# Hash attention and maxout FFN: scaling on GpSimd, one parity copied by VectorE, products of 32 columns with sums and hash in one burst, even pace, first pair by head

## The chip, the cores and the metric

The kernel runs on one core of a Trainium2 chip. The metric is the device time of one execution in microseconds, as the median of three runs: 338.43 us before the change (338.42 to 340.52). Engines are named as in the profile: PE (TensorE matmuls), PEld (its weight loads), DVE (VectorE), ACT (ScalarE), POOL (GpSimd), SP (SyncE, which here only issues DMAs).

## The reference

Attention masked by a hash, then a feed-forward network (FFN) with a maximum over three products. Batch 4, 8 heads, sequence 768, head dimension 64, six hash bits.

```python
q_bits = (np.einsum('bhsd,dk->bhsk', q, proj) > 0)      # k_bits alike
mask = q_bucket[:, :, :, None] == k_bucket[:, :, None, :]
scores = scale * np.matmul(q, k.transpose(0, 1, 3, 2))
scores = np.where(mask, scores, -1000000000.0)
attn = np.exp(scores - np.max(scores, axis=-1, keepdims=True))
attn = attn / (np.sum(attn, axis=-1, keepdims=True) + 1e-09)
attn_out = np.matmul(attn, v)
x = attn_out.transpose(0, 2, 1, 3).reshape(B * S, H * D)     # 3072 x 512
h = np.maximum(np.maximum(x @ w1, x @ w2), x @ w3)           # 3072 x 768
out = h @ w_out                                              # 3072 x 512
```

A query whose bucket holds no key of its own gets the mean of all values; the kernel has this by adding a tiny EPS times the sum of all values to the numerator and EPS times S to the denominator.

## The kernel before, in words

**Pairs.** Two heads make a pair; there are 16 pairs, four to a batch. For each pair q, k and v (384 KB each) are loaded by SP (`load`, L101, and `load_v`, L110). The sequence lies in "parity" order: a transposition (L140) puts the 64 dimensions of even chunks on partitions 0 to 63 and of odd chunks on 64 to 127.

**Preparation of a pair** (`prep_groups`, L123). Four transposition groups (`tgroup`), one for each side (q or k) and head, of three PE transposes into a PSUM tile mp and one DVE copy into T2 (L143, L145). Then `hashes` (L155): four fp32 products with the projection pj into bp, each 32 columns wide (L160), a DVE comparison to bits of +-0.5 (L163), and four small DMAs that put the bits under the dimensions in the tile S (L169). S holds 64 dimensions and 6 bits for both parities in bf16: POOL casts the even parity from T2 (L173), and an SBUF-to-SBUF DMA issued by POOL brings the odd one (L174). For pair 0 ACT writes S instead (L150, L152).

**Scores.** A unit is a pair, half of its queries, a pair of key chunks and a head: 192 units, 12 to a pair, 48 to a batch. `scores` (L221) makes two products of 70 rows into sc, and ACT takes the exponential into one of twelve fp16 tiles AT (L229). sc has two buffers, so the scores of a unit wait for the exponential of two units earlier. The bits add so much to a score that the exponential of a pair of different buckets vanishes.

**Values.** After six units (half of a pair's queries) `values` (L231) runs a burst on PE: twelve products of 64 columns into av (L237; the 385th column, of ones, gives the sum of the values), twelve of 32 columns with `ones` into sm, the denominators (L244). DVE copies both to SBUF (avs L250, ys L251). av has one buffer; sm, mp, bp and the FFN's l share three buffers named ms.

**Normalization** (`normalize`, L256), in steps at fixed distances in units after the burst: gather (at once; two SP DMAs bring the sums to dd, L271, and POOL scales the sum of the values by EPS into sv, L272), invert (6 units later; DVE adds and takes the reciprocal, and POOL issues a DMA to DRAM, rd, L275 to L278), spread (9; POOL issues two broadcasts rb, L282), scale (15 and 16; DVE computes (avs + sv) * rb into xT, L286). For the last pair of a batch each half is normalized by itself, otherwise both together.

**FFN** (`ffn_groups`, L180). For each half of a batch 18 groups of four products (three weights, six blocks of 128 columns; L190) with a DVE copy or maximum into ht (L195, L197), then three groups of six products into the output (L203), an ACT copy (L206) and an SP DMA (L208).

**Order.** All engines run their instructions in the order in which the loop at L306 emits them. For a unit u it emits in turn the loads, casts and weights that are due, the scores of u + 1, preparation, FFN groups, the burst of the six units before (one unit late), and the due steps. Preparation and FFN are paced by credits: a unit earns 0.40 of preparation (0.28 after the first batch) and 0.65 of FFN; a transposition group costs 0.34, a hash 0.82, an FFN group 0.66 or 1.32. Preparation may be up to six pairs ahead. Weights are issued by POOL at units 14, 21, 28 and 35 (L120). The FFN of a batch enters 12 units into the next. What is left runs after the loop (L338).

Of the kernel before, what the change touches and what calls it, by code (L numbers as in the profile page):

```python
# [17 lines left out]
def kernel(  # L18
# [82 lines left out]
    def load(pi):  # L101
        b, jj = divmod(pi, HPAIR)
        nats = []
        for nm, src in (("qnat", q), ("knat", k)):
            t = nat.tile([P, 2, NCH * D], FP32, tag=nm, name=nm)
            nc.sync.dma_start(t[:], src[b, 2 * jj : 2 * jj + 2].rearrange("h (p c) d -> p h (c d)", p=P))
            nats.append(t)
        natural[pi] = nats
# [14 lines left out]
    def prep_groups(pi):  # L123
        st = {}

        def begin():
            st["T2"] = t2pool.tile([P, 2, 2, HALF], FP32, tag="T2", name="T2")
            st["S"] = spool.tile([KR, 2, 2, 2, HALF], BF16, tag="S", name="S")
            trans[pi] = st["S"]
            if 2 <= pi + 2 < NPAIR:  # L130
                load(pi + 2)

        def tgroup(side, hd):
            def go():
                if not st:
                    begin()
                mp = ms_ps.tile([P, 512], FP32, tag="ms", name="mp")
                n = natural[pi][side]
                for i in range(CH2):
                    nc.tensor.transpose(mp[:, i * P : (i + 1) * P], n[:, hd, 2 * i * D : (2 * i + 2) * D], iden[:])  # L140
                o = st["T2"][:, side, hd, :]
                if side == 0:
                    nc.vector.tensor_scalar(out=o, in0=mp[:, 0:HALF], scalar1=QS, scalar2=None, op0=AluOp.mult)  # L143
# [11 lines left out]
        def hashes():  # L155
            bp = ms_ps.tile([P, 512], FP32, tag="ms", name="bp")
            for side in range(2):
                for hd in range(2):
                    g = 2 * side + hd
                    nc.tensor.matmul(bp[32 * g : 32 * g + 32, 0:HALF], pj[:, :], st["T2"][:, side, hd, :],  # L160
                                     start=True, stop=True)
            bits = bpool.tile([P, HALF], BF16, tag="bits", name="bits")
            nc.vector.tensor_scalar(out=bits[:], in0=bp[:, 0:HALF], scalar1=0.0, scalar2=0.5,  # L163
                                    op0=AluOp.is_gt, op1=AluOp.subtract)
            for hd in range(2):
                for side in (1, 0):
                    p0 = 32 * (2 * side + hd)
                    eng = nc.scalar if pi == 0 and side else nc.sync
                    eng.dma_start(st["S"][D:KR, side, hd, :, :], bits[p0 : p0 + 2 * NBITS, :])  # L169
            if pi > 0:  # L170
                so = st["S"][0:D].rearrange("d s h par w -> d (s h) par w")
                t2 = st["T2"].rearrange("p s h w -> p (s h) w")
# [3 lines left out]
        gs = [(0.34, tgroup(s, h), pi) for h in (0, 1) for s in (1, 0)]  # L176
        gs += [(0.82, hashes, pi)]
        return gs

# [38 lines left out]
    WEIGHTS_AT = (14, 21, 28, 35)  # L218
# [12 lines left out]
    def values(g):  # L231
# [15 lines left out]
        if qh == 0:  # L247
            avs_of[pi] = avspool.tile([P, 2, HALF + 4], FP32, tag="avs", name="avs")
# [7 lines left out]
    def normalize(pi, q0, nq):  # L256
# [8 lines left out]
        sv = small.tile([P, 1], FP32, tag="sv", name="sv")  # L265
# [3 lines left out]
        def gather():  # L269
            for half in range(2):  # L270
                nc.sync.dma_start(dd[:, half, 0:W], ys[32 * half : P : D, q0 : q0 + nq, :])  # L271
            nc.gpsimd.tensor_scalar_mul(sv[:], avs[:, q0, HALF : HALF + 1], EPS)  # L272

        def invert():
            nc.vector.scalar_tensor_tensor(out=rr[:, 0:W], in0=dd[:, 0, 0:W], scalar=EPS * S, in1=dd[:, 1, 0:W],  # L275
                                           op0=AluOp.add, op1=AluOp.add)
# [8 lines left out]
        def scale(i):  # L285
            return lambda: nc.vector.scalar_tensor_tensor(  # L286
                out=xt[:, jj, (q0 + i) * HALF : (q0 + i + 1) * HALF], in0=avs[:, q0 + i, 0:HALF],
                scalar=sv[:], in1=rb[:, i, :], op0=AluOp.add, op1=AluOp.mult)

        return [(0, gather), (6, invert), (9, spread)] + [(15 + i, scale(i)) for i in range(nq)]  # L290

    with tc.manual_schedule():
        load(0)
        cast_v = {0: load_v(0)}
        load(1)
        for _, g, _ in prep_groups(0):
            g()
        cast_v[0]()
        cast_v[1] = load_v(1)

        prep, ffn, steps = [], [], []
        p_credit = f_credit = 0.0
        for p2 in range(1, NPAIR):
            prep += prep_groups(p2)
        scores(0)
        for u in range(NU):  # L306
            pi = units[u][0]
            b, ub = divmod(u, UPB)
            if u % UPP == 2 and pi + 2 < NPAIR:
                cast_v[pi + 2] = load_v(pi + 2)  # L310
            if u % UPP == 8 and pi + 1 < NPAIR:
# [3 lines left out]
            if ub == 12 and b > 0:  # L315
# [19 lines left out]
        steps = [(0.85 * (n - NU), g) for n, g in steps]  # L335
        steps += [(1.35 * n, g) for n, g in values(NU // UPG - 1)]
# [35 lines left out]
```

## Time and profile before

| | |
|---|---|
| median of 3 runs | 338.43 us |
| the profiled execution's own time | 335.21 us |
| its span, first to last instruction | 333.4 us |
| mean granted TensorE clock | 0.977 |
| PE busy | 300.6 us (90%) |
| DVE busy | 180.0 us (54%) |
| ACT busy | 184.0 us (55%) |
| POOL busy | 88.4 us (27%) |
| bytes moved by DMA | 38.84 MB |

The span is cut into 40 slices in the page's second part, each digit a busy share in tenths. A group line gives busy time, the mean length of one instruction, and the idle time of the engine ahead of it with what ended it. A wait line reads: engine and line, what it waited for, total, times, longest. The chain follows the work that ended last backwards, each step to what released it.

### The profile page before, as it was taken

The page shows a single profiled execution, that of the slowest core. Times are in us where ns is not written, and L with a number is a line of the kernel's source. Part 1 is how long each engine was busy: PE and PEld are TensorE (multiplying, and loading weights), DVE is VectorE, ACT ScalarE, POOL GpSimd, SP SyncE. Part 2 cuts the span into 40 slices and gives each one's busy share as a digit, 9 for nine tenths or more (in the row PEclk, how much of TensorE's full clock was granted, in tenths as well). Part 3 has the DMA queues.
Part 4 walks back from the last instruction along what each step waited for, and adds up shares of the span by engine and source line. Part 5 has one row for each costly group of instructions (what it writes and reads, how often), then busy time and mean ns, then how long its engine had stood idle before and what let it go on. Part 6 is the DMA issues. An engine that isn't in the chain of part 4 may idle for free.

```text
span 333.4 us, 5887 instructions
## 1 busy us (share of the span) xinstructions
PE 300.6 (90%) x2192; PEld 159.2 (48%) x2192; DVE 180.0 (54%) x377; ACT 184.0 (55%) x225; POOL 88.4 (27%) x136
## 2 busy tenths in 40 slices
PE   1599993798877999999999999999999999999994
PEld 1165542253433555556545554455455545546561
DVE  1245660555425665476726674376355627768480
ACT  1576574076680567766474656777777676420202
POOL 0033272263541232323532132122313030321000
PEclk9999998599997999999999999999999999999998
DMA  5458979989783444454443214323431030141202
GB/s 179 158 192 148 214 176 230 194 255 157 251 156 94 82 139 90 163 137 129 81 114 71 52 51 108 115 49 79 104 108 46 5 139 7 50 118 27 96 0 94
DMA packets 32059, 38.84 MB, mean 117 GB/s; under 512 B 8464, under 2 KB 27936, under 8 KB 32032
## 3 DMA queue, kind: packets, MB, share of 16 engines
q1 hardware_dynamic: 22988, 25.94, 25.2%
q0 software_dynamic: 9008, 12.52, 21.3%
q8 instruction: 17, 0.28, 0.4%
q14 instruction: 10, 0.08, 0.1%
q10 hardware_dynamic: 36, 0.02, 0.0%
HBM read 31.46 MB, written 6.39 MB: 114 GB/s over the span
## 4 chain that ended last, share of the span: by engine, by line
PE 74%; DMA 11%; ACT 5%; DVE 3%; issue 3%; POOL 2%; SPq 1%; ACTq 0%; DVEq 0%; POOLq 0%
PE l L190 28%; PE sc L226 15%; PE av L237 10%; PE l L203 8%; PE sm L244 5%; DMA rb<-rd 4%; ACT AT L229 4%; PE bp L160 4%; PE mp L140 4%; DMA dd<-ys 3%; DMA rd<-rr 2%; DMA knat<-in_k_dram 1%; DVE T L145 1%; DMA S<-bits 1%; ACT osb L206 1%
## 5 line engine op out<-in xcount | busy, mean ns | idle before, releaser
L229 ACT ACTIVATE AT<-sc,bias_t 128x768 f16<-128x768 f32 x192 | 167.1, 906 | 98.9 <-PE sc L226 89.5
L190 PE MATMUL l<-xT,w_sb 128*128 128x384 f16 x576 | 111.2, 327 | 2.4 <-DVE T L145 2.4
L226 PE MATMUL sc<-S 70*128 70x384 bf16 x384 | 92.8, 330 | 11.2 <-ACT AT L229 7.5
L190 PEld LDWEIGHTS <-w_sb 128*128 128x128 f16 x576 | 55.5, 97 | 43.6 <-issue 8.2
L197 DVE TENSOR_TENSOR ht<-ht,l 128x384 f16<-128x384 f16 x96 | 53.1, 553 | 20.1 <-PE l L190 16.6
L226 PEld LDWEIGHTS <-S 70*128 70x128 bf16 x384 | 34.6, 98 | 51.5 <-issue 29.9
L195 DVE CAST ht<-l 128x384 f16<-128x384 f32 x48 | 26.7, 556 | 32.5 <-PE l L190 31.9
L278 POOL DMA_DIRECT2D rd<-rr x20 | 13.7, 684 | 115.1 <-DVE rr L277 115.1
L237 PE MATMUL av<-AT,vo 128*64 128x385 f16 x384 | 39.3, 341 | 0.0
L173 POOL CAST S<-T 64x1536 bf16<-64x1536 f32 x15 | 22.2, 1480 | 58.9 <-DVE T L143 56.5
L206 ACT COPY osb<-l 128x512 f32<-128x512 f32 x24 | 14.2, 590 | 39.6 <-PE l L203 39.6
L203 PE MATMUL l<-wout_sb,ht 128*128 128x512 f16 x144 | 34.2, 379 | 0.3 <-DVE ht L197 0.3
L250 DVE COPY avs<-av 128x385 f32<-128x385 f32 x32 | 17.9, 560 | 26.2 <-PE av L237 26.2
L282 POOL DMA_DIRECT2D rb<-rd x40 | 21.7, 545 | 30.5 <-DMA rd<-rr 28.9
L145 DVE COPY T<-mp 128x384 f32<-128x384 f32 x32 | 17.8, 555 | 21.9 <-PE mp L140 20.8
L286 DVE SCALAR_TENSOR_TENSOR xT<-avs,sv,rb 128x384 f16<-128x384 f32 x32 | 19.5, 612 | 18.2 <-DMA rb<-rd 18.2
L237 PEld LDWEIGHTS <-vo 128*64 128x64 f16 x384 | 19.6, 112 | 18.5 <-issue 10.8
L160 PE MATMUL bp<-T,pj 128*32 128x384 f32 x128 | 19.6, 542 | 7.4 <-DVE T L143 7.2
L140 PE MATMUL mp<-iden,knat 128*128 128x128 f32 x96 | 17.2, 291 | 6.9 <-DMA knat<-in_k_dram 6.9
L244 PE MATMUL sm<-AT,ones 128*32 128x384 f16 x384 | 21.6, 332 | 0.0
L203 PEld LDWEIGHTS <-ht 128*128 128x128 f16 x144 | 13.9, 97 | 15.8 <-DVE ht L197 1.1
L143 DVE TENSOR_SCALAR T<-mp 128x384 f32<-128x384 f32 x32 | 17.7, 552 | 6.2 <-PE mp L140 6.0
(28 smaller groups left out, 126.8 us busy)
## 6 DMA issues: line engine op xcount, KB each, us to landing
qnat<-in_q_dram SPq DMA_DIRECT2D x16, 384.0 KB
knat<-in_k_dram SPq DMA_DIRECT2D x16, 384.0 KB
vnat<-in_v_dram SPq DMA_DIRECT2D x16, 384.0 KB
out_dram<-osb SPq DMA_DIRECT2D x24, 256.0 KB
rb<-rd POOLq DMA_DIRECT2D x24, 192.0 KB, 3.5
S<-T POOLq DMA_DIRECT2D x15, 192.0 KB, 4.1
w_sb<-in_moe_w_dram POOLq DMA_DIRECT2D x3, 768.0 KB, 10.3
rb<-rd POOLq DMA_DIRECT2D x16, 96.0 KB, 3.0
```

What stands on the lines that cost most here:

```text
L140: nc.tensor.transpose(mp[:, i * P : (i + 1) * P], n[:, hd, 2 * i * D : (2 * i + 2) * D], iden[:])
L160: nc.tensor.matmul(bp[32 * g : 32 * g + 32, 0:HALF], pj[:, :], st["T2"][:, side, hd, :], start=True, stop=True)
L173: nc.gpsimd.tensor_copy(so[:, :, 0, :], t2[0:D])
L190: nc.tensor.matmul(ps[:, 0:HALF], w_sb[wi][:, jc, fb * P : (fb + 1) * P], xb[:, jc, hf * HALF : (hf + 1) * HALF], start=(jc == 0), stop=(j ...
L195: nc.vector.tensor_copy(hts[fb][:], ps[:, 0:HALF])
L197: nc.vector.tensor_tensor(out=hts[fb][:], in0=hts[fb][:], in1=ps[:, 0:HALF], op=AluOp.max)
L203: nc.tensor.matmul(ps[:, 0:DM], hts[fb][:, tb * P : (tb + 1) * P], wout_sb[:, fb, :], start=(fb == 0), stop=(fb == NFB - 1))
L226: nc.tensor.matmul(sc[:, j, 0:HALF], th[0:KR, 1, hd, j, kp * P : (kp + 1) * P], th[0:KR, 0, hd, qh, :], start=True, stop=True)
L229: nc.scalar.activation(at[:, :, 0:HALF], sc[:, :, 0:HALF], ActFn.Exp, bias=bias_t[:], scale=SCALE)
L237: nc.tensor.matmul(av[hd * D : (hd + 1) * D, 0 : HALF + 1], vones[pi][:, hd, c * D : (c + 1) * D], ats[2 * (c // 2) + hd][:, c % 2, 0 : HA ...
L244: nc.tensor.matmul(sm[32 * t : 32 * t + 32, 0:HALF], ones[:, :], ats[2 * (c // 2) + hd][:, c % 2, 0:HALF], start=(s == 0), stop=(s == CH2 ...
L282: nc.gpsimd.dma_start(rb[hd * D : (hd + 1) * D, 0:nq, :], rd[hd : hd + 1, 0 : nq * HALF].to_broadcast((D, nq * HALF)))
```

## The change

- The product with rb and the sum with sv: sv is now made by DVE from av itself (one column), added as a per-partition scalar in the copy of av to avs; the constant for the denominators is added in the copy of sm to ys. The product avs * rb moves to POOL (`tensor_mul`).
- The odd parity of S is copied by DVE from T2 instead of by a DMA.
- The av products are 24 of 32 columns instead of 12 of 64. A hash that is ready is emitted between the sm products and the copies of the burst, so it stands on PE right after sm, and on DVE its bits and its parity copy stand ahead of sv, avs and ys.
- Pace: one transposition group in each of the first four units of six until the FFN begins, then one in every third unit; FFN credit 0.66; FFN from 9 units into a batch; weights at units 18, 28, 38, 48; v loaded one pair ahead, not two; steps at 0, 6, 8, 10.
- Pair 0: its loads are cut by head and k comes first; proj is issued by ACT instead of by SP ahead of q and k; hash, bits and their DMAs run by head. In every pair k is loaded ahead of q.

```diff
-    for par in range(2):
-        nc.sync.dma_start(pst[par * D : (par + 1) * D, :], proj[:, :])
-        nc.vector.tensor_copy(pj[par * D : (par + 1) * D, par : 2 * NBITS : 2], pst[par * D : (par + 1) * D, :])
+    def load_proj():
+        for par in range(2):
+            nc.scalar.dma_start(pst[par * D : (par + 1) * D, :], proj[:, :])
+            nc.vector.tensor_copy(pj[par * D : (par + 1) * D, par : 2 * NBITS : 2], pst[par * D : (par + 1) * D, :])
...
+        for h0, nh in ((0, 1), (1, 1)) if pi == 0 else ((0, 2),):
+            for side in (1, 0):
+                h = 2 * jj + h0
+                nc.sync.dma_start(nats[side][:, h0 : h0 + nh, :],
+                                  (q, k)[side][b, h : h + nh].rearrange("h (p c) d -> p h (c d)", p=P))
...
+            if pi == 0:
+                for hd in hds:
+                    for side in range(2):
+                        p0 = 32 * (2 * side + hd)
+                        nc.vector.tensor_scalar(out=bits[p0 : p0 + 32, :], in0=bp[p0 : p0 + 32, 0:HALF], scalar1=0.0,
+                                                scalar2=0.5, op0=AluOp.is_gt, op1=AluOp.subtract)
+                        (nc.sync, nc.scalar)[side].dma_start(st["S"][D:KR, side, hd, :, :],
+                                                             bits[p0 : p0 + 2 * NBITS, :])
+                return
...
-                nc.gpsimd.tensor_copy(so[:, :, 0, :], t2[0:D])
-                nc.gpsimd.dma_start(so[:, :, 1, :], t2[D : 2 * D])
+            nc.gpsimd.tensor_copy(so[:, :, 0, :], t2[0:D])
+            nc.vector.tensor_copy(so[:, :, 1, :], t2[D : 2 * D])
...
+        if pi == 0:
+            return [tgroup(1, 0), tgroup(0, 0), lambda: hashes((0,)), tgroup(1, 1), tgroup(0, 1), lambda: hashes((1,))]
+        return [tgroup(s, h) for h in (0, 1) for s in (1, 0)], hashes
...
-    WEIGHTS_AT = (14, 21, 28, 35)
+    WEIGHTS_AT = (18, 28, 38, 48)
+    FFN_AT = 9
...
-                nc.tensor.matmul(av[hd * D : (hd + 1) * D, 0 : HALF + 1], vones[pi][:, hd, c * D : (c + 1) * D],
-                                 ats[2 * (c // 2) + hd][:, c % 2, 0 : HALF + 1], start=(c == 0), stop=(c == NCH - 1))
+                for vh in range(2):
+                    p0, d0 = hd * D + 32 * vh, c * D + 32 * vh
+                    nc.tensor.matmul(av[p0 : p0 + 32, 0 : HALF + 1], vones[pi][:, hd, d0 : d0 + 32],
+                                     ats[2 * (c // 2) + hd][:, c % 2, 0 : HALF + 1], start=(c == 0), stop=(c == NCH - 1))
...
+        if hash_ready:
+            hash_ready.pop(0)()
...
-        nc.vector.tensor_copy(avs_of[pi][:, qh, 0 : HALF + 1], av[:, 0 : HALF + 1])
-        nc.vector.tensor_copy(ys_of[pi][:, qh, :], sm[:, 0:HALF])
+        sv = small.tile([P, 1], FP32, tag="sv", name="sv")
+        nc.vector.tensor_scalar(out=sv[:], in0=av[:, HALF : HALF + 1], scalar1=EPS, scalar2=None, op0=AluOp.mult)
+        nc.vector.tensor_scalar(out=avs_of[pi][:, qh, :], in0=av[:, 0:HALF], scalar1=sv[:], scalar2=None, op0=AluOp.add)
+        nc.vector.tensor_scalar(out=ys_of[pi][:, qh, :], in0=sm[:, 0:HALF], scalar1=EPS * S / 2, scalar2=None,
+                                op0=AluOp.add)
...
-            return lambda: nc.vector.scalar_tensor_tensor(
-                out=xt[:, jj, (q0 + i) * HALF : (q0 + i + 1) * HALF], in0=avs[:, q0 + i, 0:HALF],
-                scalar=sv[:], in1=rb[:, i, :], op0=AluOp.add, op1=AluOp.mult)
-
-        return [(0, gather), (6, invert), (9, spread)] + [(15 + i, scale(i)) for i in range(nq)]
+            return lambda: nc.gpsimd.tensor_mul(xt[:, jj, (q0 + i) * HALF : (q0 + i + 1) * HALF],
+                                                avs[:, q0 + i, :], rb[:, i, :])
+
+        return [(0, gather), (6, invert), (8, spread)] + [(10, scale(i)) for i in range(nq)]
...
-            if u % UPP == 2 and pi + 2 < NPAIR:
-                cast_v[pi + 2] = load_v(pi + 2)
-            if u % UPP == 8 and pi + 1 < NPAIR:
+            if u % UPP == 0 and pi + 1 < NPAIR:
+                cast_v[pi + 1] = load_v(pi + 1)
+            if u % UPP == 10 and pi + 1 < NPAIR:
                 cast_v[pi + 1]()
...
-            p_credit = min(p_credit + (0.40 if b == 0 else 0.28), 0.8)
-            f_credit = min(f_credit + 0.65, 1.4)
-            while prep and p_credit > 0 and prep[0][2] < pi + AHEAD:
-                c, g, _ = prep.pop(0)
+            if prep and prep[0][0] < pi + AHEAD and (u % UPG < 4 if u < UPB + FFN_AT else u % 3 == 2):
+                _, i, g, hs = prep.pop(0)
                 g()
-                p_credit -= c
+                if i == 3:
+                    hash_ready.append(hs)
+            f_credit = min(f_credit + 0.66, 1.4)
...
-        steps = [(0.85 * (n - NU), g) for n, g in steps]
-        steps += [(1.35 * n, g) for n, g in values(NU // UPG - 1)]
+        steps = [(n - NU, g) for n, g in steps]
+        steps += [(1.3 * n, g) for n, g in values(NU // UPG - 1)]
```

More of the change, by code (lines that the diff above doesn't have):

```diff
@@ L102, in load @@
         b, jj = divmod(pi, HPAIR)
[L103 to L107, printed above, removed]
+        nats = [nat.tile([P, 2, NCH * D], FP32, tag=nm, name=nm) for nm in ("qnat", "knat")]
+        for h0, nh in ((0, 1), (1, 1)) if pi == 0 else ((0, 2),):
[3 more added lines that the diff above has]
+                                  (q, k)[side][b, h : h + nh].rearrange("h (p c) d -> p h (c d)", p=P))
         natural[pi] = nats
@@ L153, in tgroup, with hashes @@
             return go
-        def hashes():
+        def hashes(hds=(0, 1)):
             bp = ms_ps.tile([P, 512], FP32, tag="ms", name="bp")
-            for side in range(2):
-                for hd in range(2):
+            for hd in hds:
+                for side in range(2):
                     g = 2 * side + hd
@@ L162, in hashes @@
             bits = bpool.tile([P, HALF], BF16, tag="bits", name="bits")
+            if pi == 0:
+                for hd in hds:
+                    for side in range(2):
+                        p0 = 32 * (2 * side + hd)
[4 more added lines that the diff above has]
+                return
             nc.vector.tensor_scalar(out=bits[:], in0=bp[:, 0:HALF], scalar1=0.0, scalar2=0.5,
                                     op0=AluOp.is_gt, op1=AluOp.subtract)
-            for hd in range(2):
+            for hd in hds:
                 for side in (1, 0):
                     p0 = 32 * (2 * side + hd)
[L168 to L172, printed above, removed]
-                nc.gpsimd.tensor_copy(so[:, :, 0, :], t2[0:D])
-                nc.gpsimd.dma_start(so[:, :, 1, :], t2[D : 2 * D])
-        gs = [(0.34, tgroup(s, h), pi) for h in (0, 1) for s in (1, 0)]
-        gs += [(0.82, hashes, pi)]
-        return gs
+                    nc.sync.dma_start(st["S"][D:KR, side, hd, :, :], bits[p0 : p0 + 2 * NBITS, :])
+            so = st["S"][0:D].rearrange("d s h par w -> d (s h) par w")
+            t2 = st["T2"].rearrange("p s h w -> p (s h) w")
+            nc.gpsimd.tensor_copy(so[:, :, 0, :], t2[0:D])
[3 more added lines that the diff above has]
+        return [tgroup(s, h) for h in (0, 1) for s in (1, 0)], hashes
     def ffn_groups(b):
@@ L245, in values @@
                                      ats[2 * (c // 2) + hd][:, c % 2, 0:HALF], start=(s == 0), stop=(s == CH2 - 1))
+        if hash_ready:
+            hash_ready.pop(0)()
         jj = pi % HPAIR
         if qh == 0:
-            avs_of[pi] = avspool.tile([P, 2, HALF + 4], FP32, tag="avs", name="avs")
+            avs_of[pi] = avspool.tile([P, 2, HALF], FP32, tag="avs", name="avs")
             ys_of[pi] = yspool.tile([P, 2, HALF], FP32, tag="ys", name="ys")
-        nc.vector.tensor_copy(avs_of[pi][:, qh, 0 : HALF + 1], av[:, 0 : HALF + 1])
-        nc.vector.tensor_copy(ys_of[pi][:, qh, :], sm[:, 0:HALF])
+        sv = small.tile([P, 1], FP32, tag="sv", name="sv")
[3 more added lines that the diff above has]
+                                op0=AluOp.add)
         if jj == HPAIR - 1:
@@ L264, in normalize @@
         rr = small.tile([P, 2 * HALF // D], FP32, tag="rr", name="rr")
-        sv = small.tile([P, 1], FP32, tag="sv", name="sv")
         rd = drp.tile([2, 2 * HALF], FP32, tag="rd", name="rd")
@@ L271, in gather @@
                 nc.sync.dma_start(dd[:, half, 0:W], ys[32 * half : P : D, q0 : q0 + nq, :])
-            nc.gpsimd.tensor_scalar_mul(sv[:], avs[:, q0, HALF : HALF + 1], EPS)
         def invert():
-            nc.vector.scalar_tensor_tensor(out=rr[:, 0:W], in0=dd[:, 0, 0:W], scalar=EPS * S, in1=dd[:, 1, 0:W],
-                                           op0=AluOp.add, op1=AluOp.add)
+            nc.vector.tensor_add(rr[:, 0:W], dd[:, 0, 0:W], dd[:, 1, 0:W])
             nc.vector.reciprocal(rr[:, 0:W], rr[:, 0:W])
@@ L285, in scale @@
         def scale(i):
-            return lambda: nc.vector.scalar_tensor_tensor(
-                out=xt[:, jj, (q0 + i) * HALF : (q0 + i + 1) * HALF], in0=avs[:, q0 + i, 0:HALF],
-                scalar=sv[:], in1=rb[:, i, :], op0=AluOp.add, op1=AluOp.mult)
-        return [(0, gather), (6, invert), (9, spread)] + [(15 + i, scale(i)) for i in range(nq)]
+            return lambda: nc.gpsimd.tensor_mul(xt[:, jj, (q0 + i) * HALF : (q0 + i + 1) * HALF],
+                                                avs[:, q0 + i, :], rb[:, i, :])
+        return [(0, gather), (6, invert), (8, spread)] + [(10, scale(i)) for i in range(nq)]
     with tc.manual_schedule():
         load(0)
+        load_proj()
         cast_v = {0: load_v(0)}
         load(1)
-        for _, g, _ in prep_groups(0):
+        for g in prep_groups(0):
             g()
         cast_v[0]()
-        cast_v[1] = load_v(1)
-        prep, ffn, steps = [], [], []
-        p_credit = f_credit = 0.0
+        prep, hash_ready, ffn, steps = [], [], [], []
+        f_credit = 0.0
         for p2 in range(1, NPAIR):
-            prep += prep_groups(p2)
+            ts, hs = prep_groups(p2)
+            prep += [(p2, i, g, hs) for i, g in enumerate(ts)]
         scores(0)
@@ L314 @@
                 load_weights(WEIGHTS_AT.index(u))
-            if ub == 12 and b > 0:
+            if ub == FFN_AT and b > 0:
                 ffn += ffn_groups(b - 1)
```

## The prediction

> **What bounds the kernel now.** I read the slices first, then stretches, waits and the chain where the slices dip, and for prices the groups and single instructions of the timeline. A "unit" is one pair of score products with its exponential (192 in all), a "round" six units with one burst of av and sm products.
>
> ```profile
> PE   1599993798877999999999999999999999999994
> PEclk9999998599997999999999999999999999999998
> ```
> ```profile
> 47.00:67.00 20.00, 12.54 (x91) 5.29 (x88) 6.89 (x15) 5.91 (x8) 6.93 (x9) 0.74 1.06 226
> 67.00:102.00 35.00, 27.55 (x219) 14.00 (x219) 16.65 (x36) 23.95 (x30) 16.69 (x23) 1.00 0.89 208
> 150.00:290.00 140.00, 138.99 (x1073) 73.96 (x1073) 80.92 (x166) 94.46 (x113) 34.66 (x58) 1.00 0.31 78
> ```
> The columns are stretch, length, busy time of PE, weight loads, DVE, ACT and POOL, granted clock, DMA share, GB/s. From 150 to 290 us PE is busy for 138.99 of 140: there only PE's own work counts. The time that can be won lies before 102 us, and in 47 to 67 the DMA engines are full (1.06) and the clock falls to 0.74. The waits of 43 to 67 us name the engine that is held:
>
> ```profile
> ACT AT L229 <- PE sc L226: 14.0, 4, 11.9
> DVE xT L286 <- DMA rb<-rd: 7.8, 1, 7.8
> PE bp L160 <- DVE T L143: 7.0, 1, 7.0
> ```
> and the chain through that place shows the order:
> ```profile
> 35.34 7.35 DMA dd<-ys
> ...
> 46.96 0.69 POOL w_sb L120
> 47.65 0.51 POOL rb L282
> 48.16 10.78 DMA rb<-rd
> ...
> 60.11 2.96 PE bp L160 x8
> ```
> DVE stands at a scaling whose rb needs 10.78 us to land behind weights and S<-T, and T copies queue behind it, so PE and ACT stop. It happens again (3.3, 4.0 us on DVE before 94.45 and 100.82). The bursts start at 24.83, 32.29, 39.67, 46.47, 63.0 and, the last before the FFN, 92.47 and 104.94: a round of 7.4 us where nothing is late.
>
> **Prices.** Start to start in the timeline: sc pair 0.33, three transposes 0.33, l group 0.652, l2 group 1.296, bp 0.785 (+0.09 to enter), av 1.106 (six rows of two at 0.165, 0.116 to change over to sm), sm 0.604 (three rows of four at 0.165, 0.109 to leave). Exponentials follow each other by 0.785 and last 0.91, starting 0.53 after their sc. DVE copies of 384 columns: 0.56, 0.47 apart when queued.
>
> **Parts with a cost.**
> 1. *Scaling leaves DVE* (32 x 0.61 us and the waits above). POOL now waits for rb; behind it in its queue stand S copies (their T2 buffer comes back 18 units on, S is read later still), weight issues and rd of the next pair. That cover is some 20 us; were rb later, DVE's next T copy would stand for POOL's S copy. In the FFN phase DVE is 58% busy, so nothing is won there. A POOL product of 384 columns has no row: 0.42 (half of vo's 0.84 for 768) to 1.48 (its S copy of 1536); two inputs, so I take 0.84.
> 2. *S<-T off the DMA* (POOL issue 10.2 us in all, its packets 15 x 1.6 us of all sixteen engines); weights spread from 7 to 10 units. I cost the DMA relief through the waits alone. v comes one pair ahead, ten units before its cast: some 12 us for a landing, nothing.
> 3. *The odd parity on DVE*: 64x1536 fp32 to bf16, 15 times, no row. Least, the 0.17 of the 64x6 copy; most, 1.76 (four times 0.40, plus 0.16, the rate of DVE's PSUM copies). Those read PSUM and this reads SBUF; the middle, 0.96, is what I take. The Trainium skill, VectorE: DVE Perf Modes, The perf-mode tier table, gives fp32 copies inside SBUF two elements a cycle; an estimate from its 1227 ns for 2048 is also near 0.96 us, and no row of this trace shows that mode.
> 4. *av as 32-column products*: rows of four. sm already runs four at 0.165 a row; so av keeps 6 x 0.165 and the 0.116 change goes. bp joins and loses its own 0.09. Least gain nil, worst in the rivals.
> 5. *New order on DVE*: bits and the S copy now stand ahead of sv, avs and ys. In the built order the fourth transposition group after a burst takes sm's buffer and waits for ys. sv costs 0.16 (rr's 12 columns). In a burst without a hash ys ends near 2.4, ahead of the group that wants sm's buffer near 3.1: hidden by those products. The gather's SP issues move behind the four S<-bits (rival).
>
> **A round of the first stage** (burst at 0): av+sm 1.485, bp to 2.27. DVE: bits 2.40 to 2.96, S copy to 3.86, sv (0.16) 4.0, avs, ys to 5.05. PE: sc 2.27, mp 2.60, sc 2.93, mp 3.26, sc 3.75 (exponential), then mp wants 4.08 and gets 5.07; sc 5.40, 5.73; the next round's first sc waits for its exponential until 6.88, against -0.75 in this one. Round 7.63; without the ys wait 6.87; with a copy of 1.76, 8.43. So the rounds get no shorter than the undisturbed 7.4: the gain is only the two disturbed stretches.
>
> **The head.** Issues of proj (0.61, 0.57) and of the whole q tile (0.59) leave the place ahead of k. The half k tile lands near 3.7 (1.5 to 4.1 after its issue, by pst and by knat's 4.12), then transposes, T, bp (2.05 cold), two bits, issue 0.75 to 0.95, landing 1.94: first scores near 11.5 instead of 15.47. The second head's T copies stand behind the first's bits; its scores come near 15.6 instead of 16.53, and these set the exponentials. The bp of pair 1 (1.16) leaves the place ahead of the first burst: 24.83 - 0.9 - 1.2 = 22.8. Gain 0 to 4; ACT's two proj issues end before its first copy.
>
> **Sum.** Burst 0 at 22.8; pair 1's hash comes one round later and its S<-bits reach SP as four issues of 0.75, so that round takes 1 more (8.6); six more of 7.63: the burst of unit 48 at 77.2. From it batch 0's last xT half for the FFN: ys 5.05, rr 0.4, rd issue and landing 4.4 (3.1 to land in the median, 5.95 at 89.53), two rb issues and landing 4.9 (3.0 to land), product 0.84: 92.8, less 0.5 for the l products that don't need it: FFN from 92.3 (before: 101.96, three units later). POOL's issues keep that order, and other DMAs are bounded in the rivals.
> From there PE's own work: sc 134 x 0.328 = 44.0; bursts 23 x 1.70 = 39.1; l 144 x 0.652 = 93.9; l2 24 x 1.296 = 31.1; transposes 24 x 0.33 = 7.9; bp 6 x 0.785 = 4.7; together 220.7. The same count for before (130 sc pairs, 23 bursts of 1.80, 21 transposition groups, 6 bp of 0.88) is 221.2, and it took 227.14 (101.96 to 329.10): 1.7 of that slow clock after its 2.4 us wait, 0.3 a wait, 3.9 changes of form. I keep 3.9, and 1.7 for the wait ahead of the FFN. New: after three of the six late hashes (the others meet long l2 groups) an l group wants sm's buffer at 3.91 and gets it at 5.07: 3 x 1.16 = 3.5. In the tail the last batch's first xT (about 8 us after the last unit) meets 8.9 us of left-over groups, so it is covered by 0.9; without, it costs at most as much as before's 2.4 wait. End as before, 4.3.
> 92.3 + 220.7 + 3.9 + 1.7 + 3.5 + 4.3 = 326.4 against 333.4: 7.0 less. The profiled execution took 335.21 (1.8 around its span), the median of the runs is 338.43, 5.0 over the span. Forecast 331.4.
>
> **A rule that speaks against it.** POOL's S copies take 1.45 to 1.50 us beside DVE's PSUM copies, once 1.72 beside a scaling with two SBUF inputs: a loss of 0.2; by that row all 11 copies that PE may wait for cost 2, inside the range. The Trainium skill, SBUF — State Buffer, Who interferes with whom, says a VectorE copy in two-port mode and a GpSimd instruction shut each other out for a whole instruction. By that rule the sum would reach 331.4 + 16 if every copy met one of POOL's.
>
> **Rivals.**
> - *S copy near the least*: 8 x 0.76 in rounds and chain, 3 x 0.8 later: 8.5 off, 322.9.
> - *S copy at 1.76*: 8 x 0.8 + 3 x 0.8 = 8.8 more: 340.2, no change. For it: every DVE row moves a column in about 1.04 ns.
> - *dd late again*: its issue now follows four S<-bits, ending at 7.2 of a round, and invert stands at 12.7 on DVE. Its 6.75 us at 35.96 under a full DMA would be late by 1.3, four times: 5 more, 336.4. Against: a DMA share nearer 0.8.
> - *Slower: DVE's and POOL's copies block each other.* Both read the same T2 and write the same S. Where DVE's has to wait out a whole POOL copy it loses that copy's 1.48, and the loss falls on ys: 8 in rounds and chain, 3 late, 11 x 1.48 = 16.3: 347.7. It decides from 0.64 a copy. Against: POOL's copy may start after T, 6.1 in the round before, and end at 7.6; for: a wait for rb pushes it into DVE's.
> - *32-column products don't keep sm's pace*: twice the weight loads, each of another tile. At 0.184 a pair as av has now, 0.37 a row of four: 1.1 x 32 = 35 more. It decides at 0.037 a row. Against: sm's rows.
>
> **How the numbers follow.** Forecast 0.46; cheap copy 0.10; dear copy 0.13; dd late 0.11; blocked copies 0.13; slow products 0.07. About 1% is what a measurement tells from no change: 335.0 and 341.8. Faster: 0.42 of the forecast's 0.46 (own range 326 to 336), 0.10, 0.04 of dd: 0.56. Slower: 0.03 of the dear copy, 0.13, 0.07: 0.23. Same: 0.21. The range leaves out 0.07 below and 0.13 above: 322 to 345.
>
> **What would show it.** Right: no DVE wait for rb, clock 1.00 until the FFN; bursts 7.6 apart; PE idle near 1 us a round until ys; S copy 0.9 to 1.0; burst 1.5 plus bp; FFN from about 92. Wrong: rounds of 8.4 or more, an S copy that varies with POOL, av rows above 0.2, or DVE idle for dd.

## The result and the profile after

The changed kernel takes 361.4 us (median of 4 runs, 360.18 to 362.27), 1.071 times the kernel before [1.062, 1.080]: slower by 7%, where 331.4 was forecast. The profiled execution took 360.18 us, its span is 358.2 (before 333.4), its mean granted clock 0.936 (before 0.977). Ratios here and below are taken over undisturbed runs of one chip alone, so they can differ a little from the quotient of two medians.

The slices of the changed kernel, PE and its granted clock:

```profile
PE   4497888888719999899848999999799999819995
PEclk9998989898868999999969999999999999968999
```

The long dip that the kernel before had near 55 us is gone. In its place stand a row of 8s from 36 to 90 us and four holes (near 104, 184, 256 and 318 us), and with them the clock falls, at a regular beat in the first stage. The same stretches as before:

```profile
47.00:67.00 20.00, 15.90 (x148) 9.07 (x148) 11.03 (x24) 11.80 (x16) 8.58 (x10) 0.90 0.66 159
67.00:102.00 35.00, 26.98 (x256) 13.80 (x256) 17.24 (x38) 18.26 (x22) 14.95 (x17) 0.84 0.71 167
150.00:290.00 140.00, 129.02 (x1161) 71.70 (x1160) 76.55 (x163) 88.73 (x107) 47.37 (x58) 0.98 0.28 78
```

From 47 to 67 PE works 15.90 us instead of 12.54, and the DMA share is down from 1.06 to 0.66: the stall that the change aimed at is cured. But the clock in 67 to 102 is 0.84 instead of 1.00, and in 150 to 290, where PE had been busy for 138.99 of 140 us, it now stands idle for 11. The waits say for what:

```profile
PE l L201 <- POOL xT L302: 24.0, 4, 9.3
...
PE mp L144 <- DVE ys L269: 7.1, 8, 0.9
```

In the kernel before, l waited once at its first product:

```profile
PE l L190 <- DVE T L145: 2.4, 1, 2.4
```

The FFN's first products now wait four times for an xT that POOL has not made yet, 24.0 us in all. And once in each round of the first stage a transposition waits 0.9 us for ys. Over the whole span PE is idle for 52.9 us instead of 28.5, and busy at half clock for 30.2 us instead of 8.7. If half of that busy time is lost, the clock costs 15.1 us instead of 4.4 (an estimate from the clock's records); the rest of PE's time is 9.8 us shorter than before. POOL's timeline ahead of the first of the four waits (start, length, operation, and in brackets the idle time before it and what ended it):

```profile
92.72 1.96 POOL L302 TENSOR_TENSOR xT<-avs,rb 128x384 f16<-128x384 f32 x2 [5.18 <-DMA rb<-rd]
94.62 0.89 POOL L124 DMA_DIRECT2D wout_sb<-in_moe_w_out_dram  x1
95.51 1.48 POOL L184 CAST S<-T 64x1536 bf16<-64x1536 f32 x1
96.92 0.85 POOL L294 DMA_DIRECT2D rd<-rr  x1
102.73 1.07 POOL L298 DMA_DIRECT2D rb<-rd  x2 [4.97 <-DMA rd<-rr]
106.37 0.98 POOL L302 TENSOR_TENSOR xT<-avs,rb 128x384 f16<-128x384 f32 x1 [2.58 <-DMA rb<-rd]
```

The reciprocal of the batch's last pair is done at 91.23 (DVE), but its rd goes out at 96.92. It stands behind the scaling of the pair before, for which POOL waits 5.18 us until rb has landed, and behind the weight issue and the S copy that follow. From there the chain runs alone: rd lands 5.5 us on, rb 3.5, product 0.98, and the first l comes at 107.41, having been wanted at 99.77.

In the last wait the order is the same: the reciprocal is done at 308.07, and rd goes out behind a scaling. In the second wait (5.69 us, until 184.07) it is not:

```profile
171.59 0.87 POOL L294 DMA_DIRECT2D rd<-rr  x1 [0.54 <-DVE rr L293]
175.89 1.06 POOL L298 DMA_DIRECT2D rb<-rd  x2 [3.43 <-DMA rd<-rr]
183.03 0.99 POOL L302 TENSOR_TENSOR xT<-avs,rb 128x384 f16<-128x384 f32 x1 [6.08 <-DMA rb<-rd]
...
309.79 1.94 POOL L302 TENSOR_TENSOR xT<-avs,rb 128x384 f16<-128x384 f32 x2 [4.26 <-DMA rb<-rd]
311.68 0.87 POOL L294 DMA_DIRECT2D rd<-rr  x1
```

There rd goes out 0.29 us after its reciprocal (171.30), and what comes late is rb: it lands 5.94 us after the end of its issue, where the median of this kernel is 2.7. The DMA share in these 5.94 us is 0.83; which transfer holds rb no run isolates.

The second loss shows in two rounds, and in windows of 3.41 us, laid on the beat at which the clock changes:

```profile
32.26:41.76 9.50, 7.81 (x69) 4.13 (x68) 4.61 (x9) 4.92 (x7) 1.97 (x2) 0.82 0.78 196
41.76:49.79 8.03, 6.34 (x69) 3.62 (x68) 4.86 (x11) 5.16 (x7) 0.75 (x2) 0.97 0.44 116
```
```profile
45.93:49.34 3.41, 1.79 (x12) 1.16 (x12) 2.59 (x7) 2.59 (x4) 0.55 (x1) 1.00 0.14 27
49.34:52.75 3.41, 3.41 (x43) 1.67 (x45) 0.56 (x1) 1.05 (x2) 1.88 (x3) 0.50 0.96 277
```

Rounds take 8.0 to 8.5 and 9.0 to 9.5 us in turn. In the window from 45.93 PE works 1.79 of 3.41 us: the 0.90 wait for ys and the 0.72 wait for an exponential fall into it together. In the next window the granted clock is 0.50, though PE never stops in it.

### The profile page after: what moved, and what is told of

Same layout as the page of the kernel before. It is cut to its first block, busy times and chain, and to the rows that moved or that the text cites. A ratio compares the mean times of both kernels' runs of the same rounds, so it can differ in the third digit from the quotient of the medians.

```text
span 358.2 us, 6711 instructions
## 1 busy us (share of the span) xinstructions
PE 301.5 (84%) x2576; PEld 166.0 (46%) x2576; DVE 182.0 (51%) x395; ACT 185.1 (52%) x225; POOL 107.2 (30%) x133
## 4 chain that ended last, share of the span: by engine, by line
PE 63%; DMA 16%; DVE 9%; POOL 4%; issue 3%; ACT 2%; SPq 1%; ACTq 0%; POOLq 0%; DVEq 0%
PE l L201 25%; PE sc L238 12%; PE av L251 9%; DMA rb<-rd 7%; DMA rd<-rr 6%; PE l L214 5%; PE mp L144 4%; PE sm L258 4%; PE bp L164 4%; DVE S L185 3%; POOL xT L302 2%; DMA S<-bits 2%; DVE bits L176 2%; ACT AT L241 2%; DVE ys L269 2%
## 5 line engine op out<-in xcount | busy, mean ns | idle before, releaser
L201 PE MATMUL l<-xT,w_sb 128*128 128x384 f16 x576 | 116.8, 337 | 26.8 <-POOL xT L302 24.0
L238 PE MATMUL sc<-S 70*128 70x384 bf16 x384 | 94.7, 335 | 13.2 <-ACT AT L241 7.5
L201 PEld LDWEIGHTS <-w_sb 128*128 128x128 f16 x576 | 57.4, 100 | 67.8 <-issue 34.3
L302 POOL TENSOR_TENSOR xT<-avs,rb 128x384 f16<-128x384 f32 x32 | 31.8, 1007 | 53.8 <-DMA rb<-rd 53.8
L251 PE MATMUL av<-AT,vo 128*32 128x385 f16 x768 | 41.9, 357 | 0.0
L294 POOL DMA_DIRECT2D rd<-rr x20 | 13.9, 695 | 82.6 <-DVE rr L293 82.6
L184 POOL CAST S<-T 64x1536 bf16<-64x1536 f32 x15 | 24.1, 1607 | 27.0 <-DVE T L147 27.0
L251 PEld LDWEIGHTS <-vo 128*32 128x32 f16 x768 | 18.6, 101 | 18.7 <-issue 11.9
L176 DVE TENSOR_SCALAR bits<-bp 128x384 bf16<-128x384 f32 x15 | 8.4, 558 | 33.7 <-PE bp L164 33.7
L144 PE MATMUL mp<-iden,qnat 128*128 128x128 f32 x96 | 17.6, 295 | 7.1 <-DVE ys L269 7.1
L258 PE MATMUL sm<-AT,ones 128*32 128x384 f16 x384 | 23.0, 348 | 0.0
```

Source lines behind the costliest of these rows:

```text
L201: nc.tensor.matmul(ps[:, 0:HALF], w_sb[wi][:, jc, fb * P : (fb + 1) * P], xb[:, jc, hf * HALF : (hf + 1) * HALF], start=(jc == 0), stop=(j ...
L238: nc.tensor.matmul(sc[:, j, 0:HALF], th[0:KR, 1, hd, j, kp * P : (kp + 1) * P], th[0:KR, 0, hd, qh, :], start=True, stop=True)
L251: nc.tensor.matmul(av[p0 : p0 + 32, 0 : HALF + 1], vones[pi][:, hd, d0 : d0 + 32], ats[2 * (c // 2) + hd][:, c % 2, 0 : HALF + 1], start=( ...
L302: return lambda: nc.gpsimd.tensor_mul(xt[:, jj, (q0 + i) * HALF : (q0 + i + 1) * HALF], avs[:, q0 + i, :], rb[:, i, :])
```

## The experiments

Three theories were set against each other. A: the FFN starts late, because on POOL rd of a batch's last pair stands behind a scaling that waits for rb. B: the rounds of the first stage cost, because signs and copy stand ahead of ys on DVE. C: the transfers of rr and rb take longer by themselves. Every run is a whole kernel with the full computation. The new head, the later loading of v and the pace of the preparation were not undone by themselves.

| run | edit, from | median us | ratio to before |
|---|---|---|---|
| changed kernel | | 361.4 | 1.071 [1.062, 1.080] |
| e1_ffn12 | changed: FFN at 12 | 355.24 | 1.059 [1.054, 1.065] |
| e2_ys_first | changed: sums first | 354.28 | 1.058 [1.053, 1.062] |
| e3_scale_dve | changed: scaling on DVE | 401.01 | 1.199 [1.194, 1.205] |
| e4_cols32 | before: 32-column products | 333.79 | 0.990 [0.985, 0.995] |
| e5_scale14 | changed: scaling at 14 | 355.34 | 1.058 [1.048, 1.067] |
| e6_scale14_ys | e5 + e2 | 335.99 | 1.003 [0.998, 1.007] |
| e7_scale14_ys_ffn12 | e5 + e2 + e1 | 329.66 | 0.984 [0.975, 0.992] |
| e8_dve15_ys_ffn12 | e7, scaling on DVE at 15 | 328.56 | 0.979 [0.971, 0.987] |
| e9_dve15_ys_ffn15 | e8, FFN at 15 | 328.84 | 0.971 [0.966, 0.976] |
| e10_copy_by_dma | changed: odd parity by DMA | 367.39 | 1.077 [1.068, 1.086] |
| e11_weights_spread | before: weights spread | 337.36 | 1.005 [0.999, 1.011] |
| e12_scale14_ys_ffn15 | e7, FFN at 15 | 324.53 | 0.961 [0.955, 0.966] |
| e13_late_ys | e12 without e2's edit | 338.98 | 1.018 [1.008, 1.028] |
| e14_scale10 | e12 without e5's edit | 337.0 | 1.001 [0.993, 1.008] |

**FFN begun later.**

```diff
-    FFN_AT = 9
+    FFN_AT = 12
```

> The changed kernel with the FFN of a batch entering 12 units into the next instead of 9. Theory A (the time is lost where PE waits for xT at the starts of the FFN, 24.0 us in four places, because on POOL the rd and rb issues of the last pair stand behind a scaling that waits for the rb of the pair ahead): three more units of other work cover some 4 us of each of the first three waits (7.6, 5.7, 1.5) and some more groups are left over as cover for the last (9.3): waits for xT near 12 us, span near 347. Theory B (the time is lost in the rounds of the first stage, where bits and the S copy stand ahead of ys on DVE and the clock halves): the waits for xT fall but the rounds stay at 8.0 to 9.5, span 350 or more. Theory C (DMAs land later for their own reasons): the waits stay as long, span near 358.

Measured 355.24. The l products ask for xT at 102.07 instead of 99.77 and still wait until 109.39; the waits fall from 24.0 us in four to 13.5 in two, the eight ys waits of the first stage stay, and l now waits for ys too, 8.0 us in six. Some waiting is covered, its cause isn't touched.

**Sums and values first.** `hashes` returns a function that emits signs, S<-bits and both copies, and the burst calls it after ys.

```diff
-        if hash_ready:
-            hash_ready.pop(0)()
+        evac = hash_ready.pop(0)() if hash_ready else None
...
                                 op0=AluOp.add)
+        if evac:
+            evac()
```

> The changed kernel with sv, avs and ys ahead of bits and the S copy on DVE; PE's order is kept. Theory B: the waits for ys (0.9 in each of eight rounds, 1.1 twice later) go, with them the halved clock in the first stage; rounds of 7.0 to 7.4 instead of 8.0 to 9.5, the burst of unit 48 some 10 us earlier, span near 345. Theory A: the rounds shorten too, but the four waits for xT stay at 24 us or grow by what the rounds gain, since the chain on POOL is no shorter; span 350 to 356.

Measured 354.28. A round of this run (the one before it takes 6.90 us too):

```profile
47.47:54.37 6.90, 6.22 (x69) 3.66 (x68) 4.61 (x9) 4.85 (x7) 1.88 (x3) 1.00 0.82 235
```

6.90 us at full clock: B is right about the rounds, which come 8.9 us earlier in sum (burst of unit 48 at 75.90 against 84.83). But the time falls by 1.4 points only. POOL hands the gain back:

```profile
88.11 1.94 POOL L305 TENSOR_TENSOR xT<-avs,rb 128x384 f16<-128x384 f32 x2 [3.81 <-DMA rb<-rd]
90.00 1.28 POOL L124 DMA_DIRECT2D wout_sb<-in_moe_w_out_dram  x1
91.29 1.48 POOL L185 CAST S<-T 64x1536 bf16<-64x1536 f32 x1
92.69 0.85 POOL L297 DMA_DIRECT2D rd<-rr  x1
```

The reciprocal was done at 83.18; rd goes 9.5 us later, and l waits 12.43 us (from 91.5) instead of 7.64.

**Scaling on DVE, at the same place.**

```diff
-            return lambda: nc.gpsimd.tensor_mul(xt[:, jj, (q0 + i) * HALF : (q0 + i + 1) * HALF],
+            return lambda: nc.vector.tensor_mul(xt[:, jj, (q0 + i) * HALF : (q0 + i + 1) * HALF],
```

> The changed kernel with the product with rb on DVE again, at the same distances. Theory A: rd and rb of the last pair leave POOL 6 us earlier, waits for xT fall from 24 to under 10 us; DVE now waits for rb itself, up to 5 us a pair in the first stage, as before the change; span 345 to 352. Theory B or C: no gain, the wait only changes its engine, span 358 or more.

Measured 401.01, the slowest of all. At 10 units rb has not landed, and whoever scales waits for it:

```profile
DVE xT L302 <- DMA rb<-rd: 99.9, 20, 10.0
```

On DVE the T copies stand behind that wait and PE stops with them (5.6, 6.5 and 4.5 us from 54.70, 78.93 and 105.06). As A expected, the waits of l for xT fall, to 6.4 us in two; what A did not expect is this price on DVE. So the engine that carries the wait does matter: with the wait left in, POOL is the cheaper place by 13 points.

**32-column products alone,** in the kernel before.

```diff
+                for vh in range(2):
+                    p0, d0 = hd * D + 32 * vh, c * D + 32 * vh
...
```

> The kernel before with the products of 32 columns alone. If rows of four at 0.165 us and the spared change of form (0.1 us a burst) are what they bring: 32 x 0.1 = 3 us less on PE, of which 2.3 in the part where PE is the bound; 334 to 337 beside 338.4. If the loads of many tiles cost: more than 338.

Measured 0.990: the part is worth 1%. PE on the av products of the kernel before, then of this run:

```profile
L237 PE MATMUL av<-AT,vo 128*64 128x385 f16 x384 | 39.3, 341 | 0.0
```
```profile
L239 PE MATMUL av<-AT,vo 128*32 128x385 f16 x768 | 39.7, 334 | 0.0
```

Twice as many products in the same busy time, and none waits for its weights. From av to the first sm it takes 1.000 us instead of 1.106, 32 times: 3.4 us.

**Scaling behind rd.** At 14 units after the burst the scaling of a batch's third pair stands behind rd of its last (emitted 12 units after the same burst).

```diff
-        return [(0, gather), (6, invert), (8, spread)] + [(10, scale(i)) for i in range(nq)]
+        return [(0, gather), (6, invert), (8, spread)] + [(14, scale(i)) for i in range(nq)]
...
-        steps = [(n - NU, g) for n, g in steps]
+        steps = [(min(n - NU, 4), g) for n, g in steps]
```

> The changed kernel with the scalings issued 14 units after their burst instead of 10 (in the tail at most four groups in), so that on GpSimd rd of a batch's last pair stands ahead of the scaling that waits for the rb before. Theory A (the FFN starts late because rd stands in GpSimd's queue behind that scaling): rd goes out within 1 us of its reciprocal, near 92 us, the first l product comes 4 to 6 us earlier, near 102, and the four l waits for xT fall from 24 us to 8 or less: 342 to 349 us. Theory C (the transfers of rr and rb take that long whatever stands ahead of them): the waits stay above 18 us, 357 to 362. Theory B (the first stage's rounds are what costs) expects the bursts unmoved and, by itself, no gain here.

Measured 355.34, outside A's range and outside C's.

```profile
92.29 0.85 POOL L294 DMA_DIRECT2D rd<-rr  x1 [2.60 <-DVE rr L293]
...
99.37 1.48 POOL L184 CAST S<-T 64x1536 bf16<-64x1536 f32 x1
103.45 0.85 POOL L294 DMA_DIRECT2D rd<-rr  x1 [2.60 <-DVE rr L293]
104.31 1.00 POOL L302 TENSOR_TENSOR xT<-avs,rb 128x384 f16<-128x384 f32 x1
```
```profile
99.44 2.23 DVE L185 CAST S<-T 64x1536 bf16<-64x1536 f32 x1
```

rd now waits for its reciprocal and for nothing else, and goes 4.6 us earlier. But the reciprocal stands on DVE behind the late ys, no earlier than in the changed kernel (92.00 against 91.23), and the last scaling stands behind the next rd, whose reciprocal is late for the same reason (103.15). The move also brought the two S copies together: DVE's ahead of these reciprocals take 2.01 us (from 88.51) and 2.23 instead of 0.95, beside POOL's. l starts at 105.37 instead of 107.41; its waits fall to 16.5 us, not to 8, and the second of them, where rb itself is late, stays at 5.9. Neither A nor B alone is the cause: each keeps the same chain late after the other is mended.

**Both.** The two edits together, and with the FFN at 12 (the tail's bound 6 in place of 4).

> As the run before, and sums and values evacuated ahead of the hash signs and the VectorE copy of S. The kernel with that second edit alone won 7 us, of which the first stage's rounds gave 8 and the first FFN start took 5 back (its l wait rose to 12.4 us, rd standing 9.5 us behind its reciprocal). If A and B are separate costs, the two edits add: rounds of 7 to 8, rd behind its reciprocal at once near 84 us, l waiting 5 to 7 us from 91 at the first FFN start, 335 to 341 us. If only the chain's own landing times count (C), the l waits stay above 20 us and the time stays at 352 to 355.

> As the run before, and the FFN begun 12 units into the next batch instead of 9, as in the kernel before. With rd in time, xT of the last pair is ready near 97 us, when the first l product asks for it: l waits for xT together under 4 us, 328 to 335 us, that is level with or a little below the kernel before. By C the first l wait stays at 7 us or more and the time at 343 or more.

Measured 335.99 and 329.66. Alone the edits gave 1.4 points each, together 6.9; with the FFN at 12 another 1.9. So the costs don't add; they lie on one chain. The expectation had put 335 to 341 down to adding, but the two single gains together would give a ratio of 1.044, and 1.003 was measured. PE's idle time shows the same: 52.9 us in the changed kernel, 48.5 and 46.8 with one edit, 34.6 with both; and the clock's cost, by the estimate used above, 15.1, then 12.5 and 16.9, then 7.6. C falls as the cause of the slowdown: over all 20 normalizations rb lands a median of 2.7 to 2.9 us after its issue ends, and rd 1.4 to 2.2, in both kernels and in all the other runs. Single transfers do take longer: rd ahead of the first l needs 4.7 us in the changed kernel, and 5.1 (from 90.38) in the kernel before; in the second wait rb needs the 5.94 us shown above. With both edits that second wait is 1.0 us and its rb lands in 2.6.

**The scaling on DVE where the kernel before had it** (15 and 16 units, spread at 9), and the FFN at 15 on either engine.

```diff
-        return [(0, gather), (6, invert), (8, spread)] + [(14, scale(i)) for i in range(nq)]
+        return [(0, gather), (6, invert), (9, spread)] + [(15 + i, scale(i)) for i in range(nq)]
...
-    FFN_AT = 12
+    FFN_AT = 15
```

> As the run before, but with the scalings on VectorE at 15 and 16 units and the spread at 9, the kernel before's places: the rest of the change stays. If it was the place in a queue and not the engine that cost, this comes within 1.5% of the run before (328 to 338 us), GpSimd's queue being free for rd in both. If GpSimd's products are dear in themselves (0.99 us each against 0.56 on VectorE), this one is faster by 3 us or more; if VectorE's wait for rb blocks T copies as in the kernel before, it is slower by 5 us or more, with the stall between 40 and 70 us.

> The changed kernel with sums and values evacuated ahead of signs and copy, the scalings on VectorE at 15 and 16 units, the spread at 9, and the FFN begun 15 units into the next batch. With the FFN at 12 the same kernel lost 4.5 us to the first l wait (from 90.3) and 2.4 to the last one, and the idle time halved the clock for 10.2 and 3.4 us after them. Three units of scores later the first xT should be there: both waits under 1 us, the half clock after them gone, 320 to 325 us. If the transfers of rr and rb go later with the units, 326 to 330; if the FFN left over at the end costs as much as the wait saves, the same 328.

> As the run before, but the scalings on GpSimd at 14 units and the spread at 8. If the engine of the scaling makes no difference once rd is ahead of it in the queue, within 1% of the run before; if the S copies of VectorE and the products of GpSimd shut each other out often, or the products of 0.99 us count, slower by 2 to 5 us.

Measured 328.56, 328.84 and 324.53. With the queue in order the engines differ little at 12 (0.984 and 0.979, intervals that overlap), and at 15 POOL's is the better by one point, the intervals just touching. The fastest kernel beats both the changed kernel and, by 4%, the one before. Its waits on PE:

```profile
PE l L203 <- POOL xT L305: 5.8, 2, 4.8
...
PE l L203 <- DVE ys L270: 0.3, 1, 0.3
```

The expectation of 320 to 325 for the DVE version failed: DVE waits 5.9 us for an rb, until 97.89, and a transposition 3.45 us behind it, as in the kernel before; an output product waits another 4.0 us for ht, until 287.65. Its idle time is only 1.1 us above that of the fastest kernel, but the clock costs 9.4 us there against 3.6, by the same estimate.

**The odd parity by DMA again,** and **the weights spread alone,** in the kernel before.

```diff
-            nc.vector.tensor_copy(so[:, :, 1, :], t2[D : 2 * D])
+            nc.gpsimd.dma_start(so[:, :, 1, :], t2[D : 2 * D])
```
```diff
-    WEIGHTS_AT = (14, 21, 28, 35)
+    WEIGHTS_AT = (18, 28, 38, 48)
```

> The changed kernel with one part undone: the odd parity of S by GpSimd's DMA again and not by VectorE. In each round of the first stage ys then comes 0.96 us earlier: by theory B the wait of 0.90 us for it falls below 0.1, each window then holds some 0.7 us of idle time instead of 1.6, and the clock stays at 1.00 from 36 to 90 us: rounds of 7.0 to 7.8 instead of 8.0 to 9.5. The first FFN start still has rd behind the scaling: its l wait rises to 9 to 13 us and the time falls only to 352 to 357 us. If the copy were no cause, the rounds would stay at 8.0 and above and the time at 360; if the transfer's own load delays rb as in the kernel before, rounds reach 10 and the time 362 to 368.

> The kernel before with one line of the change: the four weight loads at units 18, 28, 38 and 48 instead of 14, 21, 28 and 35. The prediction's reading was that VectorE stands at a scaling from 47 to 60 us because rb lands 10.8 us late behind weights and S<-T. If the weights are what it stands behind, the stall of 7.0 us on PE and the half clock of 10.2 us after it go: 326 to 332 us. If the rest of the traffic does it, the stall moves or comes in pieces: 334 to 340.

Without DVE's copy the ys waits of PE vanish and three rounds from 40 to 62 us take 6.9 to 7.9, as B says of them. But the rounds from 62.41 and 81.04 take 10.1 and 10.9, in which av waits 5.7 us for a vo that POOL has cast late, and the time is 367.39: not the 352 to 357 of B, but the expectation's last case, the load of the transfer. The transfers of S go out on POOL's queue just ahead of rd:

```profile
100.09 0.88 POOL L294 DMA_DIRECT2D rd<-rr  x1
108.57 1.07 POOL L298 DMA_DIRECT2D rb<-rd  x2 [7.59 <-DMA rd<-rr]
```

The three rd from 60 to 105 us land 7.9, 6.9 and 7.3 us after their issue ends, where in the changed kernel they need 3.9, 2.7 and 4.7, and the l waits rise to 30.3 us. So DVE's copy spares one delay and makes another; in time the two kernels cannot be told apart (1.077 and 1.071, intervals that overlap), and that the copy alone is a gain is not shown. Spreading the weights alone does nothing measurable (1.005), which was the expectation's second case: PE's stall of 7.04 us before 60 comes back as 1.44 and 2.80, and l waits 4.27 instead of 2.39 at the FFN's start. The first rb lands 5.6 us after its issue ends instead of 10.2, so the weights did hold it, but the other waits and the clock (7.8 us instead of 4.4, by the estimate) take that back. The reading that the weights alone held rb in the kernel before was too narrow.

**Undoing one edit in the fastest kernel.**

> The fastest kernel (sums and values first, scalings on GpSimd at 14, FFN at 15) with the first of its three edits undone: signs and the VectorE copy stand ahead of ys again, as in the changed kernel. If the costs add, 6 us come back (what the edit alone won): 329 to 332 us. If the edits work through one chain, its full price shows only here, where nothing else is late: the rounds of the first stage at 8.0 to 9.5 with half clock, the first l product 8 to 10 us later, ys waits of 1.1 us in the FFN: 335 to 341 us.

> The fastest kernel with the second edit undone: scalings at 10 units, ahead of rd of the batch's last pair on GpSimd. If the costs add, 329 to 332 us. If the FFN's later begin (15 units) covers the delay of rd, 324 to 327, and the place of the scaling no longer counts. If neither, xT of the last pair comes near 104 us as in the kernel with sums first alone, the first l wait rises from 4.8 to 9 us, with more half clock behind it and the later batches' waits of 1 to 6 us back: 333 to 338.

Measured 338.98 and 337.0, both in the range of a full price. Late ys costs 5.7 points where nothing else is late, the early scaling 4.0, the FFN at 9 instead of 15 4.2 (e6 against e12, which differ in the tail's bound too); in the changed kernel each alone showed 1.2 to 1.4 (the FFN moved to 12 only). With ys late and the rest mended, l waits for xT 1.6 us in all and PE for ys 13.9: what is left there is B, made dearer where POOL's work lengthens DVE's copy (1.97 us at 54.01).

## Why the prediction was wrong

By its own steps, against the span of 326.4 that it summed:

| step | forecast | measured |
|---|---|---|
| burst 0 | 22.8 | 24.16 (+1.4) |
| from it to the burst of unit 48 | 54.4 | 60.67 (+6.3) |
| from there to the first l | 15.1 | 22.58 (+7.5) |
| from there to the end | 234.1 | 250.8 (+16.7) |

The four sum to +31.9; the spans differ by 31.8.

- *"That cover is some 20 us"* and *"POOL's issues keep that order"* failed first. The prediction named rd among the work behind the scaling and then priced it as covered. A cover holds for work that is wanted late; rd of the last pair is the head of the chain on which the FFN waits. In the third row of the table 5.7 of the 7.5 us are rd standing behind its reciprocal.
- *The waits of the last row.* Three waits of l for xT (5.69, 1.46, 9.25) make 16.4 us, where the sum had none. In the 9.25 rd stands 3.6 us behind its reciprocal (308.07 to 311.68). The other 5.8 remain when rd goes out at once (5.80 in the run with the scaling at 14), so *"covered by 0.9"* was wrong by itself: the groups left over do not last until xT comes. In the 5.69 rd was not late, but rb took 5.94 us to land; the sum had priced this chain for the first batch alone.
- That 16.4 lies so near 16.7 is chance. Behind such waits PE is busy at half clock for 13.1 us, which costs 6.5 by the same estimate, where the sum had 1.7; against it the work itself takes 220.2 us at full clock instead of 224.6.
- *The round of 7.63.* Its mechanism held to the instruction: PE waits 0.90 us for ys in eight rounds (forecast 0.99), 0.72 for an exponential, the S copy takes 0.95. What failed is the assumption of full clock, which stands only among the signs of being right. Between burst 0 and the burst of unit 48 PE is busy at half clock for 11.6 us (three windows and part of a fourth); half of it is 5.8, and 60.67 less that is 54.9, near the forecast's 54.4.
- *The head.* First scores near 12 as forecast (11.5), but the second head's bits landed late: scores wait 4.19 us from 12.58, until 16.77 (forecast 15.6), and the gain ends at 0.7 us on burst 0.
- *S copy at 0.96*: 0.94 to 0.96 in all nine copies of the first stage. That the middle of two far bounds hit it was luck. The estimate worked out from the 1227 ns for 2048 columns in the Trainium skill, VectorE: DVE Perf Modes, The perf-mode tier table, came to the same, and these rows agree with it.
- *32-column products*: rows of four at 0.165, changes as worked out; confirmed alone (0.990).
- *Late ys in the FFN phase*: 2.7 us in three waits (forecast 3.5). *POOL's product*: 0.99 us (forecast 0.84).
- *The stall of the kernel before* is gone, as forecast.
- *The rivals.* None came in. Blocked copies, the nearest in time, were not it in the changed kernel: no first-stage copy was lengthened there. They do come in other runs (scaling at 14, above). The rival that was missing is POOL's own queue, which the prediction had looked at and priced at nothing.

## What to carry to other kernels

When an operation that waits for a transfer is moved to another engine, list what stands behind it in that engine's order and ask of each when it is next wanted: an issue that heads the next chain has no cover, however long the queue's average slack. Where several delays feed one chain, undo them together before judging any: one at a time each gave 1.2 to 1.4 points, in a kernel without the others 4 to 6. And of what stands on one engine after a burst, first comes what the others wait for, here the denominators, then signs and copies. A wait on PE is priced with the half clock that may follow it.

## What the runs showed of the hardware

**Short gaps halve the clock.** The windows shown above are no accident. On the beat of 3.41 us, in fifteen of this case's sixteen profiles (all but the scaling at 10 in the fastest kernel), past 20 us, and among windows at full clock: after windows with under 1.0 us of PE idle time the next was at half clock in 0 of 1143 cases; with 1.0 to 1.3 us in 1 of 30; with 1.3 to 1.6 in 14 of 24; with 1.6 or more in 62 of 65. The idle time may be in pieces of 0.7 to 0.9 us. The head is left out for want of records: in most profiles the clock's first record lies at 20 to 23 us (22.04 in the changed kernel), and a page prints full clock ahead of it. The products say otherwise: three transposes take 0.64 us start to start there and 0.33 afterwards. The Trainium skill, TensorE: Matmul & The Clock Gate, What's actually happening, has the same window of 3413 ns and the factor of two, but puts the fall after an idle window; here some two fifths of a window idle were enough, and the measurement decides.

**DVE's copy and POOL's shut each other out.** In the run with both edits, DVE and then POOL:

```profile
80.97 4.42 DVE L186 CAST S<-T 64x1536 bf16<-64x1536 f32 x1
```
```profile
80.39 1.05 POOL L301 DMA_DIRECT2D rb<-rd  x2 [2.47 <-DMA rd<-rr]
81.44 0.84 POOL L120 CAST vo<-vnat 128x768 f16<-128x768 f32 x1
82.20 0.89 POOL L124 DMA_DIRECT2D wout_sb<-in_moe_w_out_dram  x1
83.08 1.49 POOL L185 CAST S<-T 64x1536 bf16<-64x1536 f32 x1
```

A copy of 0.95 us takes 4.42: it starts while POOL issues and ends 0.8 us after the last of POOL's four operations. Over the twelve runs in which DVE makes this copy, the 105 copies beside which POOL does nothing take 0.945 to 0.957 us; each of the longer ones, up to 4.42, overlaps POOL's work, though not each that overlaps is longer. The other way round, in the changed kernel, POOL's copy that begins at 168.86, under DVE's, takes 2.19 us instead of 1.48. Even a sum of 6 columns (rr from dd, 0.17 us) took 1.90 beside a POOL copy, in the run with the sums first. The Trainium skill, SBUF — State Buffer, Who interferes with whom, states this lock, for a whole instruction, for two-port copies and for VectorE instructions with two SBUF inputs; these rows agree, and here one copy was held over several instructions in a row. In the changed kernel it cost little, since the two copies seldom met.
